# Retention and gated MLP on one core: another stage order for the first two batches

## The chip, the core and the metric

The kernel runs on one core of a Trainium2 chip. A core has five engines with a queue each: PE (TensorE, matmuls into PSUM, with its weight loads PEld), DVE (VectorE), ACT (ScalarE), POOL (GpSimd) and SP, which here only issues DMAs. An engine runs its queue strictly in order; between engines, semaphores order the work. The metric is the device time of one execution in microseconds (us). "The clock" is the TensorE clock that was granted, as a share of full speed.

## What is computed

```python
# q, k, v: (8 batches, 8 heads, 576, 64);  x -> (8, 576, 512)
scores = scale * np.matmul(q, k.transpose(0, 1, 3, 2))
Dmat = np.where(rel >= 0, gamma[:, None, None] ** rel[None, :, :], 0.0)
attn = np.matmul(scores * Dmat, v)
x = np.ascontiguousarray(attn.transpose(0, 2, 1, 3)).reshape(B, S, H * D)
h = np.maximum(x @ w_in, 0.0)
u, v = h[..., :512], h[..., 512:]
v_n = (v - mean(v)) / np.sqrt(var(v) + 1e-06)
v_s = np.einsum('ts,bsd->btd', w_spatial, v_n) + b_spatial[None, :, None]
out = (u * v_s) @ w_out
```

## The kernel before

**Retention** (`retention(b)`, written "ret b" below) turns q, k and v of a batch into x. It goes over four chunks of 128 rows and a tail of 64 (c = 0 to 4). For each chunk `prep` scales k and q on POOL (tiles `qkv` by `kd`, `qsc` by `qs`), `scores` multiplies q by k on PE and masks the result on DVE (`at`), and `burst` does on PE the products of k and v (`ds`), of the running state and q (`qsc`), and of `at` and v. The results lie in two pairs of PSUM banks, `r`, which take turns. DVE updates the state `st`; ACT and DVE then write x as a sum of a high and a low part (a cast, and the difference to it), because every matmul of the MLP is made of three: high by high, high by low, low by high (`mm3`). The tail's x goes through a tile `xt`, which POOL copies into x.

**The MLP of a batch** has four stages on PE. v: five blocks of rows (four of 12 matmuls of 512 columns, and the tail's of 8, which reads `xt`); each is then normalized by a chain that changes between ACT and DVE (`v_steps`: relu; statistics; square root and subtraction of the mean; four small operations on `sm`; `vn` high on ACT, `vn` low on DVE). u: eight tiles of 12 matmuls of 288 columns (`u_mm`) and a relu on ACT. vs: eight tiles of 14 matmuls; DVE multiplies by u, ACT casts to `g`, DVE takes the low part. f: eight tiles of 12 matmuls, a copy on ACT, a DMA to the output. The PSUM tiles of these stages come from one pool of four banks (`ps_m`): a fifth tile waits until the first has been read for the last time.

**Weights** come in as 64-bit words and are converted on the chip into a high and a low part: `front` (ACT, then a clamp on POOL of 512 columns), `mid` (three operations on DVE), `back` (a cast on ACT, a difference on POOL). There are four such blocks of w_in for v (kind 1), four for u (kind 0) and four of w_out (kind 2); w_spatial only needs a split (`w_sp_steps`, tiles `wsp`, and `wtl` for its tail and the bias).

**What sets the order.** Up to the end of batch 0, all instructions on PE, DVE, ACT and POOL stay in the order in which the code is written (`ordered`), which is by hand: v and the u conversions lie along ret 0, then come the u tiles, then `main(0)` with vs and f of batch 0, interleaved with ret 1; w_out is converted beside vs. After it a scheduler in the compiler orders the rest. For b = 1 on, `main(b)` is v, u, vs, f, interleaved with ret b+1. The DMA queue SP waits, before each issue, for the DMA eight issues earlier to land, and for the tile to be free. `spin` issues matmuls whose result isn't used.

Of the kernel before, what the change touches and what calls it, by code (L numbers as in the profile page):

```python
# [33 lines left out]
def retention_gmlp(ctx, tc, qkv, q_x, qk_t, q_xt, v_t, w_in, w_sp, b_sp, w_out, amask, qscale, kdec, sdec, out):  # L34
# [229 lines left out]

    def retention(b):
        def burst(c, nx):
            n = rows(c)
            _, _, kn, vv = chunk[b, c]
            ps = pair().rearrange("p i (a n) -> p i a n", a=2)
            ds = ps[:, :, 0].rearrange("p r (a d) -> p r a d", a=NP)  # L270
            xo = ps[:, :, 1].rearrange("p j (a n) -> p j a n", a=2)
            if c < NC:
                for p in range(NP):
                    for r in range(2):
                        for e in (r, 1 - r):
                            h = 2 * p + side(p, e)
                            hd = slice(h * D, (h + 1) * D)
                            mm(ds[half[e], r, p], kn[half[r], hd], vv[half[r], hd], True, True)
            if c > 0:
                for p, i in heads:  # L280
                    e = side(p, i)
                    mm(xo[half[i], e, p // 2, :n], st[c % 2][half[e], p], qsc[b, c][half[e], p, :n], p < 2, False)
            if b and nx:
                scores(*nx)
            for s in range(n // D):
                for p, i in heads:
                    h = 2 * p + i
                    e = side(p, i)
                    r = half[e] if s == 0 else slice(0, n)
                    t = slice(s * D, (s + 1) * D)  # L290
                    mm(xo[half[i], e, p // 2, t], vv[r, h * D:(h + 1) * D], at[b, c][r, i, p, t], c == 0 and s == 0 and p < 2, s == n // D - 1 and p >= 2)
            t = slice(c * C, c * C + n)
            hi, lo = ((xs[b][:, i, :, t] if c < NC else xt[:, :, i]).rearrange("p (a j) n -> p j a n", j=2) for i in range(2))
            src = xo[:, :, :, :n]
            if c < NC:
                new, tmp = st[(c + 1) % 2], st[2]
                if c == 0:
                    ac.copy(out=tmp, in_=ds[:, 0])
                else:
                    ve.tensor_tensor(out=tmp, in0=ds[:, 0], in1=tmp, op=ALU.add)  # L300
                ve.tensor_tensor(out=new, in0=ds[:, 1], in1=tmp, op=ALU.add)
                if c + 1 < NC:
                    po.tensor_tensor(out=tmp, in0=new, in1=sd.broadcast_to([P, NP, D]), op=ALU.mult)
            yield 0.0
            ac.copy(out=hi, in_=src)
            ve.tensor_tensor(out=lo, in0=src, in1=hi.bitcast(F32), op=ALU.subtract)
            if c == NC:
                po.tensor_copy(out=xs[b][:, :, :, t], in_=xt.rearrange("p a i n -> p i a n"))

        xs[b] = slot(f"x_{b}")  # L310
        nxt = [(b, c) for c in range(NC + 1)] + [(b + 1, c) for c in range(2)]
        if (b, 0) not in at:
# [1 line left out]
            yield 0.95
            prep(b, 0)
            yield 0.0
        else:
            yield 0.95
        for c in range(NC + 1):
            nx = nxt[c + 1] if nxt[c + 1][0] < B else None  # L320
            if b and nx:
# [1 line left out]
            yield from burst(c, nx)
            if c + 2 < len(nxt) and nxt[c + 2][0] < B and nxt[c + 2] not in chunk:
# [1 line left out]
            if b == 0 and c < NC:
                yield 0.0
                prep(*nx)
                yield 0.0
                scores(*nx)  # L330
# [323 lines left out]
```

## Time and profile before

| | before |
|---|---|
| median of 3 runs (lowest to highest) | 561.87 us (560.63 to 561.94) |
| the profiled execution | 563.39 us |
| its span, first to last instruction | 561.6 us |
| mean granted clock | 0.982 |
| busy PE / DVE / ACT / POOL | 539.9 / 277.1 / 208.3 / 127.8 us |
| first matmul on data / first v matmul of batch 0 / of batch 1 | 7.34 / 22.67 / 115.05 us |

The span leaves 1.79 us of the profiled execution outside the first and the last instruction. All instructions are recorded under one line (70, that of the recording helper), so groups are told apart by their tiles. In rows of the timeline the columns are start, duration, engine, operation, output<-input, shape, count, and in brackets how long the engine had been idle and what released it.

### The profile page before, as it was taken

To read this page: it belongs to the slowest core of one execution; us is meant where nothing else is said; L and a number is where in the kernel's file an instruction comes from. 1 tells how busy PE (TensorE), PEld (TensorE's weight loads), DVE (VectorE), ACT (ScalarE), POOL (GpSimd) and SP (SyncE) were. 2 spreads that over 40 slices of the span, in tenths; PEclk is the share of its full clock that TensorE was granted. 3 is DMA by queue.
4 is the path that set the end of the run, shared out by engine and by line. 5 is a ranking of instruction groups with operands and counts; after the bars stand their busy time and mean duration, and the time that the engine had idled before them with its cause. 6 is when DMAs were issued, how large, how long until landed. Compare 5 with 4: busy or idle time off the path is not lost.

```text
span 561.6 us, 15328 instructions
## 1 busy us (share of the span) xinstructions
PE 539.9 (96%) x6740; PEld 501.5 (89%) x6740; DVE 277.1 (49%) x597; ACT 208.3 (37%) x451; POOL 127.8 (23%) x128
## 2 busy tenths in 40 slices
PE   6888997899999999999999999999999999999997
PEld 5667887889999899988999899998999889998997
DVE  6889576337351645338352473417454283505240
ACT  3464613236222552236322462226422362225422
POOL 3766555322112120121202121121201222000000
PEclk8999997899999999999999999999999999999999
DMA  8985151543225221343225332342214342020002
GB/s 310 372 277 190 46 182 48 184 142 118 49 95 179 78 95 49 127 147 104 85 65 197 119 94 50 106 168 76 96 48 146 130 134 77 9 75 11 2 1 85
DMA packets 37429, 64.08 MB, mean 114 GB/s; under 512 B 15345, under 2 KB 27633, under 8 KB 33394
## 3 DMA queue, kind: packets, MB, share of 16 engines
q1 hardware_dynamic: 37362, 63.10, 34.0%
q8 instruction: 53, 0.87, 0.6%
q14 instruction: 14, 0.11, 0.1%
HBM read 53.65 MB, written 9.44 MB: 112 GB/s over the span
## 4 chain that ended last, share of the span: by engine, by line
PE 83%; DVE 5%; POOL 3%; DMA 3%; issue 2%; ACT 2%; SPq 1%; ACTq 0%; POOLq 0%
PE vs L70 20%; PE f L70 17%; PE v L70 17%; PE u L70 16%; PE r L70 13%; DVE f L70 3%; DMA raw_v<-in_w_in 1%; DMA raw_s<-in_w_sp 1%; DMA qkv<-in_qkv 1%; POOL f L70 1%; SPq L70 1%; POOL win L70 1%; POOL wout L70 1%; DVE w L70 1%; POOL qkv L70 0%
## 5 line engine op out<-in xcount | busy, mean ns | idle before, releaser
L70 PE MATMUL vs<-wsp,vn 128*128 128x288 f32 x768 | 114.5, 298 | 0.0
L70 PE MATMUL f<-g,wout 128*128 128x288 f32 x768 | 107.0, 298 | 0.3 <-POOL wout L70 0.3
L70 PEld LDWEIGHTS vs<-wsp,vn 128*128 128x128 f32 x768 | 105.7, 189 | 1.1
L70 PEld LDWEIGHTS f<-g,wout 128*128 128x128 f32 x768 | 104.1, 190 | 1.0 <-POOL wout L70 0.5
L70 PE MATMUL v<-win,x 128*128 128x512 f32 x384 | 94.9, 403 | 0.0
L70 PE MATMUL u<-x,win 128*128 128x288 f32 x672 | 91.8, 296 | 0.0
L70 PEld LDWEIGHTS u<-x,win 128*128 128x128 f32 x672 | 90.1, 188 | 1.0
L70 PEld LDWEIGHTS v<-win,x 128*128 128x128 f32 x384 | 72.2, 191 | 16.9
L70 DVE TENSOR_TENSOR at<-r,am 128x1024 f32<-128x1024 f32 (+1 forms) x40 | 44.5, 1112 | 80.5 <-PE r L70 80.3
L70 POOL TENSOR_TENSOR qsc<-qsc,qs 128x512 f32<-128x512 f32 (+1 forms) x32 | 37.1, 1158 | 194.4 <-DMA qsc<-in_q_x 123.7
L70 PEld LDWEIGHTS r<-qkv 64*64 64x64 f32 x2176 | 46.9, 138 | 19.2 <-POOL qkv L70 6.5
L70 PE MATMUL r<-qkv 64*64 64x64 f32 (+1 forms) x2176 | 53.3, 238 | 10.2 <-POOL qkv L70 5.1
L70 DVE BATCH_NORM_STATS2 s<-v 128x6 f32<-128x512 f32 (+1 forms) x40 | 27.8, 695 | 70.3 <-ACT v L70 69.3
L70 ACT CAST g<-vs 128x288 fp32r<-128x288 f32 x64 | 25.6, 399 | 87.1 <-DVE vs L70 87.1
L70 ACT COPY o<-f 128x288 f32<-128x288 f32 x64 | 25.5, 400 | 72.5 <-PE f L70 72.5
L70 POOL TENSOR_TENSOR qkv<-qkv,kd 128x512 f32<-128x512 f32 x32 | 34.0, 1062 | 53.8 <-DMA qkv<-in_qkv 45.3
L70 DVE TENSOR_TENSOR g<-vs,g 128x288 fp32r<-128x288 f32 x64 | 29.3, 458 | 30.3 <-ACT g L70 30.3
L70 DVE TENSOR_TENSOR vs<-vs,u 128x288 f32<-128x288 f32 x64 | 29.6, 463 | 22.6 <-PE vs L70 22.6
L70 ACT CAST x<-r 128x512 fp32r<-128x512 f32 x32 | 18.8, 586 | 56.5 <-DVE st L70 56.3
L70 PE MATMUL r<-at,qkv 64*64 64x64 f32 (+1 forms) x1152 | 37.6, 228 | 0.0
L70 ACT ACTIVATE u<-u 128x288 f32<-128x288 f32 x56 | 22.4, 408 | 32.1 <-PE u L70 32.0
L70 PEld LDWEIGHTS r<-at,qkv 64*64 64x64 f32 (+1 forms) x1152 | 32.1, 141 | 2.3
(66 smaller groups left out, 496.5 us busy)
## 6 DMA issues: line engine op xcount, KB each, us to landing
qkv<-in_qkv SPq DMA_DIRECT2D x31, 1024.0 KB, 5.3
out<-o SPq DMA_DIRECT2D x64, 144.0 KB, 1.8
qsc<-in_q_x SPq DMA_DIRECT2D x24, 256.0 KB, 3.1
raw_v<-in_w_in SPq DMA_DIRECT2D x4, 512.0 KB, 8.4
qkv<-in_qk_t SPq DMA_DIRECT2D x8, 256.0 KB, 3.4
qkv<-in_v_t SPq DMA_DIRECT2D x16, 128.0 KB, 3.1
raw<-in_w_in SPq DMA_DIRECT2D x4, 512.0 KB, 6.8
raw<-in_w_out SPq DMA_DIRECT2D x4, 512.0 KB, 3.4
```

The lines of the kernel that those rows point to most:

```text
L70: ins = op(*args, **kw)
```

## The change

The order of batches 0 and 1 becomes v0, vs0, u0, v1, u1, f0, vs1, f1. Before vs0 only the first quarter of u0 is done (two tiles, with the one u conversion they need); it is kept in a tile `pre`. As u is not there yet, vs0 is copied to the tile `u` by ACT, and when a u tile is done, DVE does the relu and the product in one operation. The three other u conversions lie along vs0, the four of w_out along u0, v1 and u1. The high and low parts of g are made for half a batch at once (1152 columns: a cast on ACT, a difference on POOL), into x of batch 0. Ret 1 lies along vs0 and u0 alone; ret 2 begins with vs1. The eight DVE differences for g of batch 0 go.

```diff
@@ load_qsc
+        if (b, c) == (0, NC):
+            t = lent[0]
@@ load(0, 0)
+            fetch(1, 0)
+            fetch(1, 1)
             dma(t[:, :2], qkv[b, c, :, :2])
...
-    fetch(1, 0)
     load(0, 0)
-    for i in range(1, NCB):
+    for i in range(2, NCB):
         fetch(1, i)
@@ w_sp_steps
-        ve.tensor_tensor(out=wtl[1][96:97], in0=t, in1=wtl[1][r].bitcast(F32), op=ALU.subtract)
+        po.tensor_tensor(out=wtl[1][96:97], in0=t, in1=wtl[1][r].bitcast(F32), op=ALU.subtract)
@@ v_steps
             for cb in range(NCB):
+                if cb == 2 and (b, sb) == (0, 3):
+                    yield
@@ after ret 0 has begun; front, mid, back, v_steps, w_sp_steps as before
+    go(v[2], 2)
+    burst(0, NC, None)
+    go(sps, 2)
+    load(1, 1)
+    go(v[2])
+    evac(0, NC)
+    back(0, 0)
+    go(v[3])
+    go(v[4])
+    go(v[3])
+    go(v[2], 2)
+    go(v[4])
+    go(v[3])
+    go(sps)
     u = cp.tile([P, NDB, S], F32, name="u", tag="u")
...
+    pre = cp.tile([P, NDB, DM], F32, name="pre", tag="wout1")
+    for t in range(2):
+        ps = ps_m.tile([P, 512], F32, name=f"u_0_0_{t}", tag="m")[:, :HALF]
+        u_mm(0, 0, t, ps)
+        ac.activation(out=pre[:, t, :HALF], in_=ps, func=AF.Relu)
...
+    ret = retention(1)
+    go(ret)
+    go(ret)
...
+    work = u_work()
+    for t in range(2):
+        ts = slice(t * HALF, (t + 1) * HALF)
+        for db in range(NDB):
+            ps = vs_mm(0, db, t)
+            if db:
+                ac.copy(out=u[:, db, ts], in_=ps)
+            else:
+                ve.tensor_tensor(out=u[:, db, ts], in0=ps, in1=pre[:, t, :HALF], op=ALU.mult)
+            next(work, None)
+            if (t, db) in ((0, 2), (1, 1)):
+                go(ret)
+            next(work, None)
...
+    work = wout_work()
+    g0 = xs[0]
+    for t in range(2):
+        ts = slice(t * HALF, (t + 1) * HALF)
+        for db in range(1, NDB):
+            ps = ps_m.tile([P, 512], F32, name=f"u_0_{db}_{t}", tag="m")[:, :HALF]
+            u_mm(0, db, t, ps)
+            ve.scalar_tensor_tensor(out=u[:, db, ts], in0=ps, scalar=0.0, in1=u[:, db, ts], op0=ALU.max, op1=ALU.mult)
+            next(work)
+            if db == 2:
+                go(ret)
+        split(g0[:, 0, :, ts], g0[:, 1, :, ts], u[:, :, ts], po)
     ordered[0] = False
...
+    for stage in (v_stage(1), u_stage(1)):
+        for _ in stage:
+            next(work, None)
+    for _ in f_stage(0, g0):
+        pass
```

`u_work` runs front, mid and back of the u blocks 1 to 3 and `wout_work` those of w_out, a step at each `next`; `vs_mm` is the matmul part of a vs tile; `v_stage`, `u_stage`, `vs_stage` and `f_stage` are the loops of the old `main`, which now does v and u only for b > 1. Which rows land where is seen best on the engines themselves (L70 and L71 are the helper's line before and now; the number behind a name only tells tiles apart).

PE from block 3 of v0 to the first vs tile, before. The rows r<-x,win are the u tiles, r<-qkv of 64x128 and 64x64 x8 the scores, r_95<-qkv of 64x64 x16 the `ds` of a chunk:

```order
L70 MATMUL v_3_594<-win_77,x_145 128x512
...
L70 MATMUL v_4_608<-win_77,xt 128x512
...
L70 MATMUL r_96<-x_145,win_77 128x288 x2
...
L70 MATMUL r_95<-x_145,win_78 128x288
L70 MATMUL r_96<-qkv_0_521 64x128 x8
L70 MATMUL r_96<-qkv_0_521 64x64 x8
L70 MATMUL vs_0_0_810<-wsp_79,vn_348 128x288
...
L70 MATMUL vs_0_0_810<-wtl_82,vt_84 128x288
L70 MATMUL r_95<-qkv_0_521 64x64 x16
```

The same place now:

```order
L71 MATMUL v_3_575<-win_77,x_140 128x512
...
L71 MATMUL v_4_582<-win_77,xt 128x512
...
L71 MATMUL v_3_575<-win_77,x_140 128x512 x2
...
L71 MATMUL u_0_0_612<-x_140,win_77 128x288 x2
...
L71 MATMUL u_0_1_626<-x_140,win_78 128x288
L71 MATMUL r_96<-qkv_0_315 64x128 x8
L71 MATMUL r_96<-qkv_0_315 64x64 x8
L71 MATMUL r_95<-qkv_0_315 64x64 x16
L71 MATMUL r_96<-qkv_1_559 64x128 x8
L71 MATMUL r_96<-qkv_1_559 64x64 x8
L71 MATMUL r_95<-at_0_691,qkv_0_315 64x64 x16
L71 MATMUL vs_0_0_754<-wsp_79,vn_343 128x288
```

The tail block v_4 moved into the middle of v_3, six of the eight u tiles went behind vs0, and the first `ds` and the product of `at` and v of batch 1 moved ahead of the first vs tile.

POOL before that `ds`, before; the row qkv<-qkv,kd is the scaling of k that it reads:

```order
L70 TENSOR_TENSOR win_78<-f_534,win_77 128x4x128
L70 TENSOR_TENSOR win_78<-f_642,win_77 128x4x128
L70 TENSOR_TENSOR wsp_80<-raw_s,wsp_79 128x576
L70 TENSOR_TENSOR wtl_82<-raw_s,wtl_81 64x576
L70 TENSOR_TENSOR qkv_0_521<-qkv_0_521,kd 128x512
```

And now:

```order
L71 TENSOR_TENSOR win_78<-f_409,win_77 128x4x128
L71 TENSOR_TENSOR wsp_80<-raw_s,wsp_79 128x576 x2
L71 TENSOR_TENSOR wtl_82<-raw_s,wtl_81 64x576
L71 TENSOR_TENSOR wtl_82<-raw_s,wtl_82 1x576
L71 TENSOR_TENSOR qkv_0_315<-qkv_0_315,kd 128x512
```

Three u conversions (win) left this place, and the row of the bias (1x576) came from DVE.

ACT around the first relu of v1 (v_0<-v_0), before:

```order
L70 CAST xt<-r_95 128x2x2x64
L70 COPY o_1_1_1366<-f_1_1_1367 128x288
L70 COPY o_2_1_1382<-f_2_1_1383 128x288
L70 COPY o_3_1_1398<-f_3_1_1399 128x288
L70 ACTIVATE v_0_1415<-v_0_1415 128x512
L70 ACTIVATE sm_0_1433<-mv_0_1431,eps 128x1
L70 ACTIVATE v_0_1415<-v_0_1415,mv_0_1431 128x512
L70 ACTIVATE v_1_1442<-v_1_1442 128x512
```

And now, where f<-raw is the first step of a w_out conversion and x<-u the cast of g:

```order
L71 CAST wout_1046<-f_1070 128x4x128
L71 CAST x_140<-u 128x4x288
L71 ACTIVATE f_1179<-raw_1064 128x512
L71 CAST xt<-r_95 128x2x2x64
L71 CAST wout_1046<-f_1179 128x4x128
L71 CAST x_140<-u 128x4x288
L71 ACTIVATE v_0_1240<-v_0_1240 128x512
L71 ACTIVATE f_1267<-raw_1066 128x512
L71 ACTIVATE f_1356<-raw_1068 128x512
L71 ACTIVATE v_1_1270<-v_1_1270 128x512
L71 ACTIVATE sm_0_1258<-mv_0_1256,eps 128x1
```

Two w_out conversions and both casts of g now stand ahead of that relu, and the first steps of the other two conversions between it and the square root that follows.

More of the change, by code (lines that the diff above doesn't have):

```diff
@@ L263, in prep @@
             po.tensor_tensor(out=t, in0=t, in1=qs[:, :, :n], op=ALU.mult)
-    def retention(b):
[L266 to L308, printed above, removed]
@@ new lines, in retention_gmlp, with burst @@
+    xo = {}
+    def burst(b, c, nx):
+        n = rows(c)
+        _, _, kn, vv = chunk[b, c]
+        ps = pair().rearrange("p i (a n) -> p i a n", a=2)
+        ds = ps[:, :, 0].rearrange("p r (a d) -> p r a d", a=NP)
+        o = ps[:, :, 1].rearrange("p j (a n) -> p j a n", a=2)
+        if c < NC:
+            for p in range(NP):
+                for r in range(2):
+                    for e in (r, 1 - r):
+                        h = 2 * p + side(p, e)
+                        hd = slice(h * D, (h + 1) * D)
+                        mm(ds[half[e], r, p], kn[half[r], hd], vv[half[r], hd], True, True)
+        if c > 0:
+            for p, i in heads:
+                e = side(p, i)
+                mm(o[half[i], e, p // 2, :n], st[c % 2][half[e], p], qsc[b, c][half[e], p, :n], p < 2, False)
+        if nx:
+            scores(*nx)
+        for s in range(n // D):
+            for p, i in heads:
+                h = 2 * p + i
+                e = side(p, i)
+                r = half[e] if s == 0 else slice(0, n)
+                t = slice(s * D, (s + 1) * D)
+                mm(o[half[i], e, p // 2, t], vv[r, h * D:(h + 1) * D], at[b, c][r, i, p, t], c == 0 and s == 0 and p < 2, s == n // D - 1 and p >= 2)
+        if c < NC:
+            new, tmp = st[(c + 1) % 2], st[2]
+            if c == 0:
+                ac.copy(out=tmp, in_=ds[:, 0])
+            else:
+                ve.tensor_tensor(out=tmp, in0=ds[:, 0], in1=tmp, op=ALU.add)
+            ve.tensor_tensor(out=new, in0=ds[:, 1], in1=tmp, op=ALU.add)
+            if c + 1 < NC:
+                po.tensor_tensor(out=tmp, in0=new, in1=sd.broadcast_to([P, NP, D]), op=ALU.mult)
+        xo[b, c] = o[:, :, :, :n]
@@ L310, in retention, with evac @@
+    def evac(b, c):
+        src = xo[b, c]
+        t = slice(c * C, c * C + rows(c))
+        hi, lo = ((xs[b][:, i, :, t] if c < NC else xt[:, :, i]).rearrange("p (a j) n -> p j a n", j=2) for i in range(2))
+        ac.copy(out=hi, in_=src)
+        ve.tensor_tensor(out=lo, in0=src, in1=hi.bitcast(F32), op=ALU.subtract)
+        if c == NC:
+            po.tensor_copy(out=xs[b][:, :, :, t], in_=xt.rearrange("p a i n -> p i a n"))
+    def retention(b):
         xs[b] = slot(f"x_{b}")
@@ L312, in retention @@
         if (b, 0) not in at:
+            prep(b, 0)
             scores(b, 0)
[L314 to L318, printed above, removed]
+        yield 0.95
         for c in range(NC + 1):
[L320 to L321 removed]
+            nx = nxt[c + 1] if nxt[c + 1][0] < B and (b, c) != (1, NC) else None
+            if nx:
                 prep(*nx)
[L323 to L324 removed]
+            burst(b, c, nx)
+            evac(b, c)
+            if nxt[c + 2:] and nxt[c + 2][0] < B and nxt[c + 2] not in chunk:
                 load(*nxt[c + 2])
[L326 to L330, printed above, removed]
             yield 2.65
@@ L452, in interleave, with go @@
                     la = False
-    ret = retention(0)
-    def turn(n=1):
-        for i in range(n):
-            next(ret)
+    def go(gen, n=1):
+        for _ in range(n):
+            next(gen)
+    xs[0] = slot("x_0")
     front(1, 0, ve)
     mid(1, 0)
-    turn(2)
+    front(1, 1)
+    prep(0, 0)
     back(1, 0)
-    front(1, 1, ve)
     mid(1, 1)
-    front(1, 2)
+    scores(0, 0)
+    front(1, 2, ve)
+    back(1, 1)
     front(1, 3)
-    turn(2)
+    burst(0, 0, None)
+    mid(1, 2)
+    evac(0, 0)
     load(0, NC)
-    for i in range(NDB):
-        fetch(0, i)
-    fetch_wsp()
-    load_qsc(0, NC)
-    back(1, 1)
-    mid(1, 2)
-    spin("idle1", 6)
-    turn(2)
+    fetch(0, 0)
+    prep(0, 1)
+    spin("idle1", 3)
+    scores(0, 1)
     back(1, 2)
     mid(1, 3)
+    burst(0, 1, None)
     back(1, 3, ve)
-    spin("idle2", 2)
-    turn(4)
+    fetch_wsp()
+    evac(0, 1)
+    load(1, 0)
+    for i in range(1, NDB):
+        fetch(0, i)
+    prep(0, 2)
+    scores(0, 2)
     vn = [cp.tile([P, NC, DH], F32R, name=f"vn{i}", tag=f"vn{i}") for i in range(2)]
```

151 lines of the change are left out of this document (70 added, 81 removed).

## Prediction

> **What bounds the kernel now.** First the windows by stage; a row gives length, busy PE, PEld, DVE, ACT, POOL, the granted clock, DMA share and GB/s.
>
> ```profile
> span 561.6 us, 15328 instructions
> 7.34:62.09 54.75, 45.67 (x641) 38.17 (x641) 42.62 (x77) 27.89 (x55) 35.38 (x29) 0.91 0.80 277
> 62.09:115.05 52.96, 45.53 (x722) 43.06 (x722) 30.94 (x48) 16.04 (x35) 26.19 (x23) 0.90 0.40 130
> 180.15:245.24 65.09, 65.09 (x842) 61.05 (x841) 30.15 (x69) 23.51 (x52) 11.17 (x12) 1.00 0.32 108
> ```
>
> From 115.05 on PE never stops and the clock is 1.00: nothing can be won there but PE work, and the change removes none. The first 115 us hold the loss, in idle PE and a clock of 0.90. How much PE work they hold is told by the chain of waits, whose pieces (start, length, what) are pure PE later on:
>
> ```profile
> 180.31 5.60 PE v L70 x24
> ...
> 505.11 13.05 PE v L70 x56
> 518.16 12.73 PE u L70 x96
> 530.89 14.88 PE vs L70 x112
> 545.77 12.74 PE f L70 x96
> ```
>
> The last batch, without a ret beside it, takes 53.40 us, a middle batch 65.09: a ret is 11.69. Before v1 begins, v, u, vs, f of batch 0 and two rets have run, 76.8 us of work in 115.05: 38.3 lost. The change reorders exactly this stretch, so I walk the new queues through it with the durations of the old rows, and count PE idle and slow clock.
>
> **Up to the tail of ret 0: nothing.** Fetching the second v block of w_in ahead of q and k makes the first scores later by one transfer of 512 KB, but v0 starts when the fourth block is converted, and that stays. In my walk chunks 1 and 2 come 0.5 us earlier (one ACT copy and one POOL difference less ahead of them), and then `front(0, 0)`, now ahead of the x of chunk 2, gives that back. The spins that go stood in waits of PE.
>
> **The tail block waits for xt (+).** PE and DVE here, before:
>
> ```profile
> 29.12 3.06 PE L70 MATMUL v<-win,x 128*128 128x512 f32 x12
> 32.11 0.69 PE L70 MATMUL r<-qkv 64*64 64x64 f32 x32
> 39.15 0.46 PE L70 MATMUL r<-qsc,st 64*64 64x64 f32 x16 [1.67 <-POOL qsc L70]
> 39.77 4.61 PE L70 MATMUL v<-win,x 128*128 128x512 f32 x12
> 44.22 2.00 PE L70 MATMUL v<-win,xt 128*128 128x512 f32 x8
> ```
>
> ```profile
> 41.68 0.42 DVE L70 TENSOR_TENSOR xt<-r,xt 128x256 fp32r<-128x256 f32 x1 [1.21 <-ACT xt L70]
> 42.02 0.15 DVE L70 RECIPROCAL sm<-sm 128x1 f32<-128x1 f32 x1
> ...
> 43.73 0.75 DVE L70 SCALAR_TENSOR_TENSOR vn<-v,sm,vn 128x512 fp32r<-128x512 f32 x1 [0.82 <-ACT vn L70]
> 44.40 1.45 DVE L70 TENSOR_SCALAR f<-f 128x512 int32<-128x512 int32 x1
> ```
>
> xt was done at 42.10, hidden by block 3. Now the normalization of block 1 (four sm operations, ACT's vn, DVE's vn; 42.02 to 44.40 shows such a set: 2.4 us) stands between the tail's `at` and xt. Less 0.8 that the bursts before come earlier and the f operations run clear of POOL, xt comes at 43.7. PE begins block 3 at 38.6 (39.77 before; the tail's q no longer stands behind two clamps on POOL) and reaches v_4 after only six matmuls, at 40.1: **3.6 idle**. Queued behind v_4 are the second half of block 3, both u tiles and everything after.
>
> **What an idle PE costs behind it.** The same two sets of matmuls, warm, and after 2.93 us of idleness:
>
> ```profile
> 74.59 0.69 PE L70 MATMUL r<-qkv 64*64 64x64 f32 x32
> ...
> 75.55 0.85 PE L70 MATMUL r<-qkv 64*64 64x128 f32 x32
> ...
> 78.87 0.43 PE L70 MATMUL vs<-wtl,vt 128*128 128x288 f32 x2
> ...
> 85.95 1.13 PE L70 MATMUL r<-qkv 64*64 64x64 f32 x32 [2.93 <-DVE x L70]
> ...
> 92.80 0.43 PE L70 MATMUL vs<-wtl,vt 128*128 128x288 f32 x2
> ```
>
> 4.28 us warm, 6.85 cold: 2.6 more. After the 1.67 of idleness at 37.5, block 3 took 4.45 from start to start where block 1 took 2.99: 1.5 more. I charge 2.6 for an idle stretch of 2.9 us and longer, and 2.0 for one between.
>
> So v_4 and the half block (14 matmuls of 0.233 from 5.60/24: 3.3) end at 43.7 + 3.3 + 2.6 = 49.6, the two u tiles (2 × 12.73/8 = 3.2) at 52.8.
>
> **The first ds of batch 1 waits for POOL (+).** Before, six more u tiles (9.5 us) filled PE while ACT, DVE and POOL finished vn and w_spatial; now PE does the scores (0.85) and stands at `ds`, which needs the scaled k. The durations, from the same chain before:
>
> ```profile
> 60.41 0.30 ACT L70 ACTIVATE sm<-mv,eps 64x1 f32<-64x1 f32 x1 [0.97 <-DVE mv L70]
> 60.62 0.63 ACT L70 ACTIVATE v<-v,mv 64x512 f32<-64x512 f32 x1
> 61.19 0.69 ACT L70 ACTIVATE u<-r 128x288 f32<-128x288 f32 x2
> 61.77 1.25 ACT L70 ACTIVATE vt<-v,sm 64x512 fp32r<-64x512 f32 x2
> 62.91 1.37 ACT L70 CAST wtl<-raw_s 128x576 fp32r<-128x576 f32 x2
> ...
> 63.66 1.43 POOL L70 TENSOR_TENSOR wtl<-raw_s,wtl 64x576 fp32r<-64x576 f32 x1 [3.96 <-ACT wtl L70]
> 64.31 1.40 DVE L70 TENSOR_TENSOR wtl<-raw_s,wtl 1x576 fp32r<-1x576 f32 x1 [0.51 <-ACT wtl L70]
> ...
> 66.66 1.36 PE L70 MATMUL r<-qkv 64*64 64x64 f32 x64 [0.44 <-POOL qkv L70]
> ...
> L70 ACT CAST wsp<-raw_s 128x576 fp32r<-128x576 f32 x4 | 2.6, 666 | 0.0
> L70 POOL TENSOR_TENSOR qkv<-qkv,kd 128x512 f32<-128x512 f32 x32 | 34.0, 1062 | 53.8 <-DMA qkv<-in_qkv 45.3 <-PE f L70 7.9 <-issue 0.6
> ```
>
> ACT, whose queue has the two copies to `pre` ahead, goes on at 53.2: square root and mean for two blocks (0.78 each, 60.41 to 61.19), a wsp cast 0.67, vn 0.65, vt 1.14, wtl 1.37: 58.6. POOL takes the first wtl at 57.9 (1.43), then the row of the bias, which it has never done: between 0 and 1.43, and I take 1.43, since DVE's 1.40 for that row is no less than POOL's for 64 rows; then k, 1.1: 62.0. PE has been **idle 8.3**, where before it got to `ds` at 66.66 with vs 0,0 and six more u tiles behind it.
>
> **From there to v1: covered.** PE still has vs 14.88, six u tiles 9.55 and ret 1 without its first scores, 10.84: 35.3, plus 2.6 cold: v1 begins at 99.9. Beside it lie three u conversions. By the same walk each x of ret 1 is ready some 1.5 us before PE wants it, k and q too (an estimate); the dropped differences for g (eight of DVE) make the room. If DVE is slower there, each burst waits; that is a rival. Replacing g's casts by copies to u costs ACT the same; the new DVE operation (relu and product) I put at the 0.46 of the old product.
>
> ```profile
> L70 DVE TENSOR_TENSOR vs<-vs,u 128x288 f32<-128x288 f32 x64 | 29.6, 463 | 22.6 <-PE vs L70 22.6
> L70 POOL TENSOR_TENSOR win<-early,win 128x512 fp32r<-128x512 f32 x3 | 3.9, 1291 | 0.1
> L70 POOL TENSOR_SCALAR f<-f 128x512 f32<-128x512 f32 x8 | 12.4, 1553 | 4.3 <-ACT f L70 4.3
> L70 DVE SCALAR_TENSOR_TENSOR f<-raw,f x16: 691/694/1823, 34.3 to 99.6; 128x512 int32<-128x512 int32 x16
> 118.11 0.58 ACT L70 ACTIVATE v<-v 128x512 f32<-128x512 f32 x1 [2.42 <-PE v L70]
> ...
> 122.14 0.73 DVE L70 SCALAR_TENSOR_TENSOR vn<-v,sm,vn 128x512 fp32r<-128x512 f32 x1
> ```
>
> **v1 waits for a bank (+).** Its relu stands on ACT behind both casts of g, and the second of these behind this chain: cast of the first half (1152 columns; between 0.67 for 576 and twice that, taken 1.2), POOL's difference for it (between 1.29 for 512 columns and 2.9; 512 and 576 differ by 2.2 ns a column, so 2.7), POOL's clamp of the next w_out block 1.5, DVE's three operations and xt 2.3, the last u product 0.46, the second cast 1.2: 9.4 us. It starts when DVE has multiplied u 3,0, which I put 2.5 us before v1 (possible: 0 to 5; DVE comes to it late, behind a w_out conversion whose fetch SP issues only after the tail of batch 1). So that relu starts at 106.8 instead of 102.7. Its bank was free 4.8 us after the relu's start before (118.11 to 122.87); with two `front` steps between I take 6.5: 113.3. PE, done with four blocks (11.2) at 111.1, is **idle 2.2**; v_4 and a u tile take 3.4 plus 2.0 cold, and seven u tiles 11.1: u1 ends at 129.9, 4.2 later than its 25.8 us of work.
>
> **The sum.** f0 12.74: 142.6. Then vs1, f1 and ret 2 with one set of scores more (14.88 + 12.74 + 11.69 + 0.85): 182.8. From here all is as it was from 180.31 to 561.6: 381.3. Span 564.1 against 561.6, so +2.5; with the 1.79 outside it, 565.9 against this execution's 563.39. That execution stands 1.5 above the median, so on the scale of the runs I forecast 561.87 + 2.5 = **564.4**, the three waits eating what the shorter way to vs0 gives. About 0.3% (1.7 us) is what a measurement of this kernel can tell from no change.
>
> **Rivals.** (1) v1 gets its bank in time: if POOL's wide difference costs the 1.29 of 512 columns, or the first product comes 5 us ahead, the relu starts 2.5 to 3 us earlier, and wait and cold of v1 go: 564.4 − 4.2 = 560.2. For it: the one width that was never run decides. Against: rows grow by the column. (2) The clock holds. All three waits carry 7.2 us of cold matmuls; if the clock stays up behind them, 557.2, faster. It decides at the first idle stretch of 3.6 us. Against: idle 2.93 and even 1.67 were paid before. A half case: it holds behind v1's shorter wait alone, 562.4. [...] (3) DVE slows beside POOL in vs0. Its 16 f operations take from 0.69 to 1.82 us (the slow ones with POOL at work); six of them at the slow end, 6.8 us more, use up the 1.5 us of room at two bursts: some 4 us, 568.4. That the order isn't what is said is excluded by the queues shown.
>
> **How the numbers follow.** Forecast as walked (562 to 567) 0.46; bank in time 0.18; clock holds 0.14 for all, 0.06 for v1; DVE slower 0.10; something else 0.06. Range 557 to 569: it leaves out the lower half of the second rival, the upper half of the third and most of the rest, under 0.2. Faster by over 0.3% (below 560.2): 0.14, half of the first rival and some of the rest, 0.25. Within: the other half, the half case and the low end of the forecast, 0.23. Slower (above 563.6): 0.52.
>
> **What would show it.** In the profile after: PE idle of 3 to 4 us before v<-win,xt near 40, released by DVE xt; 8 us before r<-qkv near 54, released by POOL qkv; 2 us near 111, released by DVE vn; a clock clearly under 1 behind each; no PE wait over 1 us in vs0. It is wrong if the wait for POOL is under 5 us, if v1 starts before 95, or if vs1 and f1, which I let run unhindered, show waits.

## The result, and the profile after

| | before | after |
|---|---|---|
| median (lowest to highest) | 561.59 us (560.63 to 561.94, 4 runs) | 569.99 us (568.36 to 571.00, 4 runs) |
| ratio, 95% interval | | 1.0150 (1.0122 to 1.0178) |
| the profiled execution / its span | 563.39 / 561.6 us | 569.64 / 567.9 us |
| first v matmul of batch 1 | 115.05 us | 105.32 us |
| first v matmul of batch 2 | 180.15 us | 186.39 us |

The change makes the kernel 8.4 us slower by the medians; the two profiled executions differ by 6.3 us of span, and it is these 6.3 that the traces explain (the profiled execution of before stood 1.8 us above its median, that of after 0.35 below). Forecast were +2.5, and 564.4 us with a range of 557 to 569. From batch 2 on both traces agree within 0.1 us. The windows of after by stage: up to vs 0,0, to v1, to the end of u1, to batch 2 (columns as in the windows of before: start:end, length, busy PE, PEld, DVE, ACT, POOL, clock, DMA share, GB/s); the first row is the whole stretch.

```profile
7.69:186.39 178.70, 155.33 (x2196) 142.04 (x2196) 92.23 (x185) 65.91 (x134) 78.39 (x68) 0.93 0.47 157
7.69:65.44 57.75, 39.13 (x691) 32.15 (x692) 35.18 (x71) 24.31 (x47) 31.40 (x28) 0.85 0.62 219
65.44:105.32 39.88, 36.16 (x541) 34.86 (x537) 20.60 (x34) 11.48 (x22) 20.26 (x17) 0.92 0.55 175
105.32:132.96 27.64, 26.60 (x153) 23.48 (x153) 16.77 (x47) 17.43 (x35) 16.81 (x13) 0.99 0.11 41
132.96:186.39 53.43, 53.43 (x819) 51.55 (x817) 19.68 (x34) 12.69 (x30) 9.93 (x11) 1.00 0.44 138
```

The same stretch of before:

```profile
7.34:180.15 172.81, 156.30 (x2201) 142.28 (x2202) 103.83 (x194) 67.49 (x141) 74.23 (x65) 0.94 0.50 167
```

PE is busy 1.0 us less than before and idle 23.4 us instead of 16.5 (length less busy). So what was lost is waiting, all of it ahead of 133 us. The waits of PE in after, from its timeline (in brackets idle time and releaser):

```profile
32.64 0.69 PE L71 MATMUL r<-qkv 64*64 64x64 f32 x32 [2.08 <-POOL qkv L71]
46.11 2.11 PE L71 MATMUL v<-win,xt 128*128 128x512 f32 x8 [3.39 <-DVE xt L71]
61.88 2.41 PE L71 MATMUL r<-qkv 64*64 64x64 f32 x64 [8.25 <-POOL qkv L71]
81.49 0.69 PE L71 MATMUL r<-qkv 64*64 64x64 f32 x32 [1.84 <-DVE x L71]
101.79 0.46 PE L71 MATMUL r<-qsc,st 64*64 64x64 f32 x16 [1.88 <-DVE x L71]
121.75 11.38 PE L71 MATMUL u<-x,win 128*128 128x288 f32 x84 [0.99 <-POOL f L71]
```

The second, third and sixth are those of the prediction; the first, fourth and fifth are not in it. Where the fourth comes from is shown by DVE and POOL just ahead of it, in after:

```profile
74.98 1.05 POOL L71 TENSOR_TENSOR qkv<-qkv,kd 128x512 f32<-128x512 f32 x1
75.06 1.26 DVE L71 TENSOR_SCALAR f<-f 128x512 int32<-128x512 int32 x1 [3.50 <-POOL f L71]
...
75.98 1.49 POOL L71 TENSOR_TENSOR qsc<-qsc,qs 128x512 f32<-128x512 f32 x1
76.35 1.67 DVE L71 SCALAR_TENSOR_TENSOR f<-raw,f 128x512 int32<-128x512 int32 x1
...
80.65 0.69 DVE L71 TENSOR_TENSOR x<-r,x 128x512 fp32r<-128x512 f32 x1 [0.71 <-ACT x L71]
...
107.41 0.43 DVE L71 TENSOR_SCALAR f<-f 128x512 int32<-128x512 int32 x1 [4.67 <-POOL f L71]
107.87 1.42 DVE L71 SCALAR_TENSOR_TENSOR f<-raw,f 128x512 int32<-128x512 int32 x2
```

DVE's two steps start 0.08 and 0.37 us later than a POOL operation and end 0.29 and 0.55 us after it. They take 1.26 and 1.67 us where the last two rows, with POOL idle beside them, have 0.43 and 0.71. Why they take longer beside POOL no run shows. Behind them stand the `at`, `st` and `x` of a chunk of ret 1, for which PE waits.

The kernel before has the same pattern, POOL's scalings of k and q beside a conversion on DVE:

```profile
78.72 1.06 POOL L70 TENSOR_TENSOR qkv<-qkv,kd 128x512 f32<-128x512 f32 x1
79.72 1.48 POOL L70 TENSOR_TENSOR qsc<-qsc,qs 128x512 f32<-128x512 f32 x1
```

```profile
78.80 1.26 DVE L70 TENSOR_SCALAR f<-f 128x512 int32<-128x512 int32 x1 [1.48 <-POOL f L70]
80.09 2.39 DVE L70 SCALAR_TENSOR_TENSOR f<-raw,f 128x512 int32<-128x512 int32 x2
```

They stand ahead of the `at`, `st` and `x` for which PE waited 2.93 us at 85.95. The prediction uses that wait as a price for idleness and doesn't carry it over.

The fifth hangs on a transfer. ACT's first step of w_out, which stands ahead of the last `x` of ret 1, waited for it, and the fetch was issued at 88.50, with three others:

```profile
94.17 0.68 ACT L71 ACTIVATE f<-raw 128x512 f32<-128x512 f32 x1 [3.42 <-DMA raw<-in_w_out]
```

```profile
88.50 2.28 SPq L71 DMA_DIRECT2D raw<-in_w_out  x4
```

### The profile page after: what moved, and what is told of

The parts are those of the page before. It is cut to its first block, busy times and chain, and to the rows that moved or that the text cites. A ratio compares the mean times of both kernels' runs of the same rounds, so it can differ in the third digit from the quotient of the medians.

```text
span 567.9 us, 15304 instructions
## 1 busy us (share of the span) xinstructions
PE 539.2 (95%) x6735; PEld 501.3 (88%) x6735; DVE 266.1 (47%) x588; ACT 207.2 (36%) x445; POOL 132.7 (23%) x131
## 4 chain that ended last, share of the span: by engine, by line
PE 84%; POOL 5%; DVE 4%; DMA 3%; ACT 2%; issue 1%; SPq 0%; POOLq 0%; ACTq 0%; DVEq 0%
PE vs L71 20%; PE f L71 18%; PE u L71 17%; PE v L71 15%; PE r L71 14%; POOL f L71 2%; DVE f L71 2%; DMA qs<-in_qscale 2%; DMA am<-in_amask 1%; POOL x L71 1%; POOL qsc L71 1%; POOL qkv L71 1%; DVE st L71 1%; ACT x L71 1%; DVE at L71 0%
## 5 line engine op out<-in xcount | busy, mean ns | idle before, releaser
L71 PE MATMUL vs<-wsp,vn 128*128 128x288 f32 x768 | 114.1, 297 | 0.0
L71 PE MATMUL u<-x,win 128*128 128x288 f32 x768 | 106.6, 298 | 1.0 <-POOL f L71 1.0
L71 PEld LDWEIGHTS vs<-wsp,vn 128*128 128x128 f32 x768 | 105.2, 188 | 1.2
L71 PEld LDWEIGHTS u<-x,win 128*128 128x128 f32 x768 | 104.2, 190 | 2.3 <-POOL f L71 1.2
L71 PE MATMUL v<-win,x 128*128 128x512 f32 x384 | 94.1, 400 | 0.0
L71 PE MATMUL f<-g,wout 128*128 128x288 f32 x672 | 92.3, 296 | 0.0
L71 PEld LDWEIGHTS f<-g,wout 128*128 128x128 f32 x672 | 89.8, 188 | 0.5
L71 DVE TENSOR_TENSOR at<-r,am 128x1024 f32<-128x1024 f32 (+1 forms) x40 | 44.5, 1112 | 93.4 <-PE r L71 93.4
L71 PEld LDWEIGHTS v<-win,x 128*128 128x128 f32 x384 | 71.8, 190 | 16.8
L71 POOL TENSOR_TENSOR qsc<-qsc,qs 128x512 f32<-128x512 f32 (+1 forms) x31 | 36.3, 1171 | 175.8 <-DMA qsc<-in_q_x 99.6
L71 PEld LDWEIGHTS r<-qkv 64*64 64x64 f32 x2176 | 48.4, 141 | 25.8 <-POOL qkv L71 15.3
L71 PE MATMUL r<-qkv 64*64 64x64 f32 (+1 forms) x2176 | 54.9, 242 | 17.0 <-POOL qkv L71 13.1
L71 DVE BATCH_NORM_STATS2 s<-v 128x6 f32<-128x512 f32 (+1 forms) x40 | 27.8, 694 | 59.4 <-ACT v L71 58.4
L71 ACT COPY o<-f 128x288 f32<-128x288 f32 x64 | 25.6, 400 | 72.0 <-PE f L71 71.9
L71 ACT CAST g<-vs 128x288 fp32r<-128x288 f32 x56 | 22.3, 399 | 75.8 <-DVE vs L71 74.7
L71 POOL TENSOR_TENSOR qkv<-qkv,kd 128x512 f32<-128x512 f32 x32 | 33.3, 1044 | 41.6 <-DMA qkv<-in_qkv 27.3
L71 ACT CAST x<-r 128x512 fp32r<-128x512 f32 x32 | 18.7, 585 | 60.7 <-DVE st L71 60.7
L71 PE MATMUL r<-at,qkv 64*64 64x64 f32 (+1 forms) x1152 | 38.8, 232 | 0.0
L71 DVE TENSOR_TENSOR g<-vs,g 128x288 fp32r<-128x288 f32 x56 | 25.6, 457 | 26.3 <-ACT g L71 26.3
L71 DVE TENSOR_TENSOR vs<-vs,u 128x288 f32<-128x288 f32 x56 | 26.0, 464 | 23.1 <-PE vs L71 23.0
L71 PEld LDWEIGHTS r<-at,qkv 64*64 64x64 f32 (+1 forms) x1152 | 33.2, 145 | 2.5 <-DVE at L71 0.2
L71 POOL TENSOR_TENSOR st<-st,sd 128x256 f32<-128x256 f32 x24 | 14.7, 614 | 87.2 <-DVE st L71 87.2
```

Of the source, the lines that this page charges most:

```text
L71: ins = op(*args, **kw)
```

## The experiments

All edits are to the changed kernel. Ratios are to the kernel before, measured beside each (its medians lay between 561.48 and 561.80). "ds" is the first product of k and v of batch 1.

| run | edit | median us | ratio (95% interval) |
|---|---|---|---|
| the change | | 569.99 | 1.0150 (1.0122 to 1.0178) |
| e1 | k of batch 1 scaled early | 567.34 | 1.0099 (1.0075 to 1.0123) |
| e2 | w_out fetched early | 569.63 | 1.0137 (1.0122 to 1.0153) |
| e3 | ret 1 ahead of conversions | 568.06 | 1.0110 (1.0093 to 1.0127) |
| e4 | first u clamp later | 568.96 | 1.0127 (1.0112 to 1.0143) |
| e7 | spins in the wait | 569.37 | 1.0153 (1.0132 to 1.0173) |
| e9 | two more u tiles ahead of vs0 | 571.49 | 1.0183 (1.0167 to 1.0198) |
| e10 | e1, and first mask early | 570.58 | 1.0169 (1.0145 to 1.0193) |
| c1 | e2 + e3 | 567.30 | 1.0109 (1.0092 to 1.0126) |
| f0 | relus of u late on ACT | 569.05 | 1.0126 (1.0108 to 1.0143) |
| f1 | e1, f0's relus and e10's mask, both a little later, and splits of w_spatial early | 564.62 | 1.0049 (1.0035 to 1.0064) |
| f4 | c1 + last u product early | 575.02 | 1.0236 (1.0205 to 1.0268) |
| f2 | f1 + e2 + e3 + e4 + product early | 566.44 | 1.0079 (1.0066 to 1.0093) |
| f3 | f1 + e2 + e3 + e4 | 558.56 | 0.9943 (0.9928 to 0.9958) |
| g2 | f3, g's differences on DVE | 565.63 | 1.0085 (1.0063 to 1.0107) |
| g5 | g2 + product early | 562.50 | 1.0019 (1.0004 to 1.0033) |
| g4 | g2 + block 3 whole | 562.94 | 1.0026 (1.0013 to 1.0039) |
| g3 | f3 + block 3 whole | 556.54 | 0.9917 (0.9903 to 0.9932) |

### The two waits that were not foreseen: e2, e3, c1

```diff
@@ wout_work                                  # e2
-        for i in range(NMB):
+        for i in range(1, NMB):
             fetch(2, i)
...
+    fetch(2, 0)
     work = u_work()
@@ the vs tiles of batch 0
-            next(work, None)                 # e3
             if (t, db) in ((0, 2), (1, 1)):
                 go(ret)
+            next(work, None)
             next(work, None)
```

> Edit: the DMA of the first w_out block is issued before the vs stage of batch 0 instead of behind ret 1, together with the three others. Theory (PE's wait of 1.88 us for DVE's x at 99.9 us hangs on the fetch that landed 7.3 us after its issue, ahead of the last x of ret 1 on ACT and DVE): the wait and some 2 us of slow matmuls behind it go, v1 begins at about 101.5 instead of 105.3, span 3 to 4 us shorter. Rival (DVE's three f operations are the delay, whatever the fetch does): the wait stays over 1 us, span within 0.7.

> Edit: at the two places in vs of batch 0 where a chunk of ret 1 is issued, it stands ahead of both conversion steps of that tile instead of between them. Theory (PE's wait of 1.84 us at 79.7 us comes from DVE's two slow f operations, 1.26 and 1.67 us, ahead of the chunk's at, state and x): wait and the 1.5 us of slow matmuls behind it go, span about 3.3 us shorter, unless the conversions then come too late for u 1,0. Rival (DVE and ACT are simply full here and the same work is late elsewhere): another wait of 1 us and more in front of u0, span within 0.7.

> Edit: the early fetch of the first w_out block and the chunk of ret 1 ahead of the conversion steps, both. Theory (the stretch from the first vs tile to v1 was lost to these two waits): no wait of PE over 0.5 us between 66 and 100 us; v1 begins 38 us or less after the first ds against 43.4 with the change alone; behind it the wait at v1's tail, absent with the change alone because v1 began late, comes to 1.6 to 2.5 us plus 1.0 at the second u tile. Span 3 to 4 us shorter than the change alone. Rival (the two waits only stand in for one that comes later anyway): span within 2 of the change alone, as for the later k order by itself.

Each edit took out its own wait (e2 has none at ret 1's tail, e3 none at its chunk 2), and c1 both. By the medians e2 won only 0.4 us of the 3 to 4 expected, and e3 1.9 of 3.3. In their traces the stretch from ds to v1 is 3.2 and 5.1 us shorter, but v1's tail block then waited 1.00 and 1.59 us, and ds itself stood 2.3 and 2.0 us later than in after. The stretch from ds to v1, after and in c1:

```profile
61.88:105.32 43.44, 39.72 (x633) 38.24 (x633) 21.67 (x34) 11.48 (x22) 22.43 (x19) 0.89 0.50 161
```

```profile
64.54:101.89 37.35, 37.35 (x633) 35.97 (x633) 20.62 (x34) 11.41 (x22) 21.17 (x19) 0.94 0.56 177
```

6.1 us shorter, without any idle time. Yet the time fell by only 2.7 (3 to 4 expected): v1, begun earlier, now waited where it had not (the first of these rows; the second wait is in after too). PE in c1:

```profile
114.84 2.12 PE L71 MATMUL v<-win,xt 128*128 128x512 f32 x8 [1.59 <-DVE vn L71]
...
119.52 11.38 PE L71 MATMUL u<-x,win 128*128 128x288 f32 x84 [0.99 <-POOL f L71]
```

So in the change itself this wait was hidden only because v1 came 5 us late. ds of the profiled execution of c1 also stood 2.7 us later than that of after; the rows for that stand in the last section.

### What makes ds wait 8.25 us: e1, e9, e10, f0, f1

```diff
@@ e1: POOL scales the first k of batch 1 early
     back(0, 0)
+    prep(1, 0)
     go(v[3])
...
@@ e9: u conversion 1 there as well, and
-    for t in range(2):
+    for k in range(4):
...
@@ f0: relus behind the square roots of blocks 3 and 4
         u_mm(0, 0, t, ps)
-        ac.activation(out=pre[:, t, :HALF], in_=ps, func=AF.Relu)
+        pu.append(ps)
     go(v[4])
     go(v[3])
+    for t in range(2):
+        ac.activation(out=pre[:, t, :HALF], in_=pu[t], func=AF.Relu)
```

> Edit: POOL scales the first k of batch 1 right behind the last w_in difference for u0, ahead of the splits of w_spatial, instead of behind them. Theory (the 8.25 us in which PE stands at the first ds of batch 1 belong to that one place in POOL's queue): ds follows the scores at about 53.6 us, PE next stands at the product of at and v or at vs 0,0, which needs the w_spatial tail that POOL ends near 60.7 now and about 59.7 with one operation less ahead; so the long wait splits, PE does ds and the second scores (2.3 us) before it, and the span falls by 2 to 4 us. Rival (the chain behind is just as late, and what is done early is paid for in the next wait): under 1 us.

> Edit: the second quarter of u0 (its conversion and two tiles, 3.2 us of PE) goes back ahead of vs0, as part of what stood there before the change; two tiles fewer come after vs0. Theory (the 8.25 us at the first ds are missing cover: ACT, DVE and POOL need that time for vn and w_spatial whether PE works or not): the wait falls by 3.2 us less what the conversion adds to POOL's queue (a clamp of 1.5 and a difference of 1.3), so the first ds comes up to 2.8 later, the wait stays near 7 to 8, and two tiles of u are done by then; span 0 to 3 us shorter. Rival (the engines, not PE, are the bound of the whole stretch up to v1, so cover placed anywhere changes nothing): span longer by 1 to 3.

> Edit: as the run with the early scaling of k, and the first scores and the mask (at) of batch 1 stand on PE and DVE ahead of the last normalization steps of v0. Theory (with k early, PE's next wait of 5.19 us is for a bank that DVE's at frees, and at stands behind the normalization only by its place in the queue): PE runs through ds, the second scores and at times v at about 57 us, and the only wait left there is that of vs 0,0 for the w_spatial tail from POOL (62.9 in that run): span another 2 to 3 us shorter, 564 to 565.5. Rival (the tail of w_spatial comes later as at now delays the normalization on DVE by its 1.2 us): span within 0.7 of the run with k alone.

> Edit: on ACT the two relus of the first u tiles (into pre) stand behind the square root and mean of the last two blocks of v0 instead of ahead of them; nothing else moves. Theory (PE's wait at the first ds was 8.25 us in every run, whatever went before, since the chain of ACT, DVE and POOL that it waits for begins only when PE has done the second u tile, whose relu stands ahead of it on ACT; cover by PE work placed ahead can't shorten it): the chain begins about 2 us earlier, at the end of the statistics, and the wait falls to 6 to 6.6 us; span about 1.9 us shorter. Rival (the chain is bound by DVE or by the w_spatial splits on POOL): wait stays at 8.0 or more, span within 0.5.

> Edit: that, and the k of batch 1 scaled early, the first scores and mask ahead of the normalization's last steps, and the w_spatial splits on ACT and POOL ahead of the normalization, where both stood idle. Theory (8.25 us is the length of one chain of places in three queues, not of work: taken apart, it fits beside the u tiles): no wait of PE over 1.5 us between 53 and 66 us; vs 0,0 ends at 60 to 61.5 against 65.4; span 4 to 6 us shorter than the change alone, 564 to 566. Rival (what vs 0,0 needs comes no earlier, since the statistics of the last blocks come from PE's end of v0): vs 0,0 at 64 or later, span within 1.5 of the change alone.

In e1 the wait became 5.19 us for DVE's `at`, and the time fell by 2.7 us: what was wanted was early, the next in the queue late. In e9, with 3.2 us more of PE work ahead, the wait was as long as ever, here in e9:

```profile
68.62 2.42 PE L71 MATMUL r<-qkv 64*64 64x64 f32 x64 [8.26 <-POOL qkv L71]
```

It is 8.25 or 8.26 in after, e2, e3, e4, c1, f4 and e9. The reason is on ACT, in after:

```profile
52.84 0.41 ACT L71 ACTIVATE pre<-u 128x288 f32<-128x288 f32 x1 [1.19 <-PE u L71]
53.15 0.28 ACT L71 ACTIVATE sm<-mv,eps 64x1 f32<-64x1 f32 x1
```

The relu of the last u tile stands ahead of the square root, so the chain to ds begins when PE has done its last work ahead of ds: no amount of work there covers it. That is why e9 failed (it lost 1.5 us; its theory allowed a gain of 0 to 3, the rival's loss is what came). With the relus behind the square roots (f0) the wait fell to 6.79 us (6 to 6.6 expected) and the time by 0.9 (1.9 expected). e10 missed its 564 to 565.5 and came out 3.2 us above e1, worse than its rival as well: `at` and k were early, but vs 0,0 then waited 2.27 us for POOL's tail of w_spatial, and v1 waited 2.32 at a u tile. f1, which also puts the splits of w_spatial where ACT and POOL had stood idle, left 0.89 and 0.64 of the 8.25 and took 5.4 us off the change, although the wait at ret 1's chunk 2 grew from 1.84 to 3.58 us. PE in f1:

```profile
57.77 0.90 PE L71 MATMUL r<-qkv 64*64 64x128 f32 x32 [0.89 <-DVE at L71]
60.16 1.86 PE L71 MATMUL vs<-wsp,vn 128*128 128x288 f32 x12 [0.64 <-DVE vn L71]
```

### The clamp in ret 0, and the clock: e4, e7

```diff
-    front(0, 0)                              # e4
     evac(0, 2)
     prep(0, 3)
+    front(0, 0)
@@ e7: behind the first scores of batch 1
+    for i in range(28):
+        pe.matmul(banks[1][:, 0], wsp[0][:, 0, :P], wsp[0][:, 0, :512], start=True, stop=True)
```

> Edit: the first step of the u0 conversion (ACT, then POOL's clamp) stands behind the x of chunk 1 and the scaling of chunk 3 instead of ahead of both. Theory (PE's 2.08 us wait at the ds of chunk 3, at 32.6 us, comes from that clamp): the wait goes and ret 0's tail comes 2 us earlier, as does the normalization ahead of xt; span 2 to 2.5 us shorter. Rival (xt and then the chain to the first ds of batch 1 set the time, whenever PE gets there): the wait for xt or for POOL's k grows by what is won, span within 0.7.

> Edit: 28 matmuls of 512 columns whose result isn't used go to PE behind the first scores of batch 1, ahead of its first ds; no other instruction moves. Theory (an idle stretch of PE is paid a second time in slow matmuls behind it, about 1.2 us behind the 8.25 us wait): the clock beside and behind stays up, the stretch from the first ds to vs 0,0 (3.6 us after the change) takes 2.3 to 2.6, span 1 to 1.3 us shorter. Rival (the slow start is of the matmuls themselves and the clock has nothing to do with it): span within 0.5.

e4 took out the wait of 2.08 us, but ret 0's tail then waited 1.76 for an `x` and the tail block still 2.72 for xt: 1.0 us won, half of what was expected. In e7 the spins filled all of the wait but 1.75 us, and from ds to vs 0,0 PE took 2.14 us instead of the 3.56 that after took at a granted clock of 0.55; the mean clock was 0.988 in e7 and 0.978 in after. With the wait filled the matmuls behind it weren't slow. The time fell by only 0.6 us (1 to 1.3 expected), less than its executions spread: v1, earlier by 2.8 us in that trace, waited 1.60 us at its tail block, where the change has no wait.

### v1, and a version that beats both: f4, f2, f3, g2, g5, g4, g3

```diff
@@ f4, f2, g5: the second w_out conversion behind the last u product
-            next(work)
+            if (t, db) != (1, 2):
+                next(work)
@@ g2, g5, g4
-        split(g0[:, 0, :, ts], g0[:, 1, :, ts], u[:, :, ts], po)
+        split(g0[:, 0, :, ts], g0[:, 1, :, ts], u[:, :, ts], ve)
...
@@ g4, g3: block 3 of v0 whole
-                if cb == 2 and (b, sb) == (0, 3):
-                    yield
```

> Edit: early w_out fetch and the chunk ahead of the conversion steps as before, and in u0 the three DVE operations of the second w_out conversion stand behind the tail's xt and the last u product instead of ahead of them. Theory (the wait of 1.59 us at the tail of v1 comes from the second cast of g, which stands behind that u product, and the product behind POOL's wide difference and clamp): the cast comes 4 us earlier, the waits of 1.59 and 0.99 go; span 2.3 to 2.6 us below the run with fetch and order, 564.7 to 565. Rival (ACT's two further w_out steps ahead of the first relu, or POOL, hold the bank back all the same): a wait of 1 us or more stays, span within 1.

> Edit: all of these, and the u0 clamp behind the scaling of chunk 3. Theory (the new stage order is sound and the loss lay in these five places of the queues): the gains add up, 8 to 11 us of waits and slow matmuls less than the change alone: 559 to 562, level with the kernel before or faster. Rival (the same ACT, DVE and POOL work is the bound of the first 100 us in any order, so a wait removed comes back elsewhere): 564 or more.

> Edit: all the changes of places together, but with the second w_out conversion ahead of the last u product again as in the change (without the step that brought a wait of 6.7 us in v1). Theory (the gains up to v1 add up): v1 begins at 94 to 95 as in that run, the waits at v1 are 1.6 and 1.0 as with fetch and order alone, span some 3.5 to 5.5 us below it: 560.5 to 563, level with the kernel before. Rival (v1's conversions and normalization are so late by then that the wait grows to what was won): 565 or more.

> Edit: the same, and the two differences of 1152 columns for g go from POOL to DVE. Theory (the wait at v1's tail is the chain through POOL: 2.7 us of wide difference ahead of the clamp ahead of DVE's conversion ahead of the last u product): clamp 2.7 us earlier, no wait over 0.5 us at v1, span 1.5 to 2.5 below the run with the differences on POOL. Rival (DVE is then the late engine, two operations of some 1.5 us more stand ahead of the statistics): the waits of 1.6 and 1.0 stay or grow, within 0.5 or slower.

> Edit: the run with all changes that lost 6.7 us in v1 (last u product ahead of the second w_out conversion), with the two wide differences on DVE instead of POOL. Theory (there DVE's conversion stood still beside POOL's wide difference: one operation of two SBUF inputs took 3.04 us where it takes 0.69 alone): with no wide operation on POOL it runs at 0.7, the wait of 6.75 us falls under 1, time within 1 of the run with the differences on DVE. Rival (the 6.75 us come from the order on ACT and DVE by itself): a wait of 4 us or more stays at the first u tile of batch 1.

> Edit: differences on DVE, and block 3 of v0 whole again ahead of the tail block, as in the kernel before. Theory (PE reaches the tail block 1.4 us later, so its wait for xt falls from 2.4 to about 1.0; what was won by the early half has no use since DVE sets xt): the u tiles end 1.4 us earlier, span 0.7 to 2 us shorter than with block 3 split. Rival (the normalization of the tail block, now behind that of block 3, takes over as what vs 0,0 waits for): span within 0.5 or longer.

> Edit: the run of 558.56 us (all changes of places, differences on POOL, second w_out conversion where the change has it), and block 3 of v0 whole again ahead of the tail block. Theory (the wait for xt of 3.39 us is a loss that the split of block 3 makes; it fell to 1.99 and the time by 2.7 us when the split was undone with the differences on DVE): wait 2.0, first ds 1.2 to 1.4 us earlier, v1's waits unchanged at 1.6 and 1.0; span 1.2 to 2.7 us shorter, 556 to 557.4. Rival (the gain there was in v1's waits, not in xt): within 0.5 of 558.56.

f4 got rid of both waits at v1 and found one of 6.73 us at the first u tile; f2 has one of 6.75 there. So both missed by far: f4 took 575.02 where 564.7 to 565 were expected, f2 566.44 where it was 559 to 562. DVE there, in f4:

```profile
106.28 4.49 DVE L71 SCALAR_TENSOR_TENSOR f<-raw,f 128x512 int32<-128x512 int32 x2
110.70 0.68 DVE L71 BATCH_NORM_STATS2 s<-v 128x6 f32<-128x512 f32 x1
```

Two operations of 0.69 took 4.49 us beside POOL's wide difference (2.84) and a scaling of k (1.50), and the statistics of v1's first block stood behind them. I took this for the cause; g2 and g5 bear it out only in part. g5 is f2 without the wide operation on POOL: the same two take 2.43 us there and the time is 3.9 us shorter, but 4.37 us of wait stay, at the tail block. And g2, which should have gained 1.5 to 2.5 us that way, lost 7.1 against f3, with 6.07 of wait at the first u tile. What f4, f2, g2, g4 and g5 share is the order from v1 on, which the compiler's scheduler sets: DVE's rows of f4 and f3 behind the last u product (f_1294 is the third w_out conversion, s_1_1 and s_1_2 are statistics of v1; in f3 no row of that conversion comes up to the third row):

```
L71 BN_STATS s_1_1_1281<-v_1_1267 128x6
...
L71 TENSOR_SCALAR f_1294<-f_1294 128x512
...
L71 SCALAR_TENSOR_TENSOR f_1294<-raw_1066,f_1294 128x512
...
L71 BN_STATS s_1_2_1311<-v_2_1297 128x6
```

```
L71 BN_STATS s_1_1_1284<-v_1_1270 128x6
...
L71 BN_STATS s_1_2_1314<-v_2_1300 128x6
...
L71 SCALAR_TENSOR_TENSOR vn_344<-v_0_1240,sm_0_1258,vn_343 128x512
```

In the five, the last two conversions of w_out stand among the normalization of v1, and so they do in e9 and e10, with 2.58 and 2.32 us of wait at a u tile; in the change and the other runs they stand behind most of it. Why the scheduler drew them forward isn't shown. Whether their place alone or their slowness beside POOL costs the 4 to 7 us of the five was not separated: no run held them back.

f3, with all edits that held and v1 as in the change, took 558.56: better than its 560.5 to 563, and 3.0 us less than the kernel before. g4 and then g3 undid the split of block 3: 2.7 and 2.0 us less than g2 and f3, with xt's wait at 1.99 instead of 3.39 (1.0 and 2.0 expected). g3 is 5.2 us faster than the kernel before, 13.5 faster than the change, and does the same work in the same stage order. The stretch to batch 2 in g3, idle 13.9 us and at a clock of 0.97:

```profile
8.16:173.09 164.93, 151.08 (x2195) 137.58 (x2196) 92.10 (x185) 65.44 (x134) 78.61 (x68) 0.97 0.50 171
```

## Why the prediction was wrong

The direction was right, and so was what sets the time (PE's waits ahead of batch 2); the size was not. The forecast for the median was 564.4 us within 557 to 569, and 569.99 came. Of these 5.6 us the traces explain 3.8, 564.1 of span forecast and 567.9 measured; the rest is that the profiled execution of before stood 1.5 us above the median from which the forecast started, and that of after 0.35 below its own.

- **"Up to the tail of ret 0: nothing"** was wrong by 2.4 us: the tail block began at 46.11, not at 43.7. `front(0, 0)`'s clamp kept POOL from the k of chunk 3 (2.08 us of wait); e4 shows it, and also that only half comes back.
- **"The tail block waits for xt"**: 3.39 measured, 3.6 said. The 2.6 of slow matmuls charged behind it were 0.2 in this execution (14 matmuls in 3.51; 6.15 in c1, with the same instructions up to there), which by luck cancelled the point above: the u tiles ended at 52.7, forecast 52.8. g3 shows the split of block 3 as the price: 2.0 us.
- **"The first ds of batch 1 waits for POOL"**: 8.25 against 8.3, ds at 61.88 against 62.0. The row of the bias took what I had taken, POOL's two differences for the tail together 2.87; but DVE's 1.40, from which I took it, ended 0.62 us after the POOL operation beside it and said little of POOL, so that is luck. The walk had the chain begin behind the two copies to `pre` and took this as given; that it is order, and that all but 1.5 of the 8.25 us go with it, f0 and f1 show.
- **"From there to v1: covered"** is the step that failed: 43.44 us against 37.9, so 5.5 too little. Idle time was 3.72 (said: none) and PE's work took 39.72 instead of 37.9. I had spaces of 1.5 us at each burst as an estimate and put DVE slower beside POOL among the rivals, with 0.10. The wait at chunk 2 has the cause of the 2.93 us in the kernel before (the rows of 78.72 to 80.09 above), whose price I took and whose place I left out of the walk. The late fetch of w_out I had counted only where it delays the products ahead of v1, not for the last `x` of ret 1, which stands behind it on ACT and DVE. e3 and e2 took out one of the two waits each; c1, with both gone, takes 37.35, 3.7 us of waiting and 2.4 of slow matmuls less. So the sum was right for a stretch without them.
- **"v1 waits for a bank"**: the two costs were right (POOL's wide difference 2.65 us, said 2.7; the cast 1.15, said 1.2), but as v1 began 5.4 us late, only 1.8 of the 4.2 came, 0.99 of it as a wait at the u tiles. In c1, e1 and f3 v1 begins earlier and the wait is 1.6 plus 1.0, said 2.2; the 2.0 of slow matmuls behind it came in none of them.
- **The rest**: f0, vs1, f1 and ret 2 took 53.43, said 52.9; from batch 2 on 381.5, said 381.3.

Added up: 2.4 − 2.4 − 0.1 + 5.5 − 2.4 + 0.5 + 0.2 gives 3.7 of the 3.8 us.

The first rival (a bank in time) happened to v1, for another reason than the one given; the second (the clock holds) fails behind the 8.25 us, where 3.56 us stand against 2.14 in e7. At the place that it named as decisive, the wait for xt, the clock stayed at 1.00 in this execution and the 14 matmuls behind took 3.51 us; in c1 they took 6.15. Its half case, at v1's shorter wait of 1.59, came in c1, e1 and f3, where the 8 matmuls behind took 2.11 to 2.12 us. The third was there, at two operations instead of six.

## What to carry to other kernels

When a stage is moved, the waits that count are at the places where a short operation stands in its engine's queue behind one that waits for the engine it should overtake: here a relu of PE's last tile ahead of a chain that PE needs next. Such a wait keeps its length when work is put ahead of it (8.25 us in seven kernels, in e9 with 3.2 us more work), so look for the order of the queues before adding cover; f1 to g3 turned a loss of 1.5% into a gain of 0.8% with the same stages and the same work. And waits in a row don't add up one by one: taking out one shows what stands behind it. e2, e3, e4 and f1 brought 0.4, 1.9, 1.0 and 5.4 us alone and 11.4 together in f3; the 3.58 us that f1 had at ret 1's chunk 2 are gone there. A wait that the old trace shows belongs in the walk of the new order, unless a row says why it goes.
